# Loading keys and values over 128 partitions and regrouping the pooling and routing work of an attention and experts kernel

## The chip, the cores and the metric

The program runs on one core of a Trainium2 chip. The metric is the device time of one execution in microseconds. The core has five engines that run their own instruction queues in order: TensorE (PE in the profile, its weight loads PEld), VectorE (DVE), ScalarE (ACT), GpSimd (POOL) and SyncE (SP), which here only issues DMAs. Sixteen DMA engines move the data.

## What is computed

Attention with pooled keys and values, then a top-1 mixture of experts on its output. All tensors are float32.

```python
# q, k, v: batch 8, heads 8, sequence 576, head size 64; pool = 8, so 72 pooled keys
k_p = k.reshape(B, H, Sp, pool, D).mean(axis=3)
v_p = v.reshape(B, H, Sp, pool, D).mean(axis=3)
scores = scale * np.matmul(q, k_p.transpose(0, 1, 3, 2))
attn = softmax(scores)                      # max subtracted, sum + 1e-9
x = np.matmul(attn, v_p)                    # to 4608 tokens of 512
# experts: 8, hidden 1024
logits = x @ w_gate
expert_idx = np.argmax(logits, axis=1)      # gate_w: its softmax probability
out[mask] = gate_w[mask, None] * (np.maximum(x[mask] @ w1[e], 0) @ w2[e])
```

## The kernel before, in words

The program has two stages. `attention` computes x, finds the expert of each token and scatters the token rows, sorted by expert, to a DRAM tensor `xs` ("dispatched" in the profile). `experts`, which the change does not touch, reads these rows back in units of up to 512 tokens and multiplies them with the experts' weights, each split into a high and a low part.

Attention runs in 4 groups (g) of two batches each, and each group in 9 tiles of 128 tokens, so 36 tiles (t; i is the tile within the group). A group's k and v are each loaded in three thirds: `kv_load(g, i)` (L127 to L134) loads third i // 2 of k (i even) or v (i odd). The tile `raw` has 128 partitions of 3 x 512 floats, 786 KB in all: each partition holds 24 tokens of one head. Today this is two DMAs of 64 partitions on SP's queue, one for even and one for odd heads (`hp`), and four raw buffers are cycled. `kv_pool` (L136) adds up the 8 tokens of each pooled key in three halving adds: 128x768 (L141), 128x384 (L149) and then 64x192 into `kvp` for each hp (L146). Today GpSimd does thirds 0, 2, 3 and 5 of the next group in tiles 0 to 3, with VectorE doing the last add for hp = 1; VectorE does thirds 1 and 4 and all of group 0 but the third 3. VectorE's adds are cut into pieces in the list `halves`, of which one is taken at two points of each tile. `kv_transpose` (L156) turns a third of kvp on TensorE into the bank pm, and ScalarE copies it into kT and vT (L167, L169). `v_expand` multiplies v with a matrix that holds the identity and the gate weights, so that attention also yields each head's share of the router's logits.

A tile t of the loop does, in this order on each engine: transposes the weights P of tile t (`p_transpose`); `scores(t + 2)` on TensorE, then VectorE's row maximum mx (L224) and difference sd (L227); `q_transpose(t + 3)`; perhaps a kv_transpose or a v_expand; ScalarE's exp (`weights(t + 2)`, L232); `weigh(t)` on TensorE into the bank pU; `scale(t)` on VectorE: reciprocal (L264), logits lh (L266) and token rows xe (L268); `q_copy(t + 4)` on ScalarE (L207) from the loaded q tile `qa`. Between VectorE's operations `weave` takes steps from the list `steps`.

These steps are the routing. Tokens are routed in batches of three tiles (the last two batches have two tiles and one). When a batch's last tile is done (i = 2, 5, 8), `route` (L281) puts its steps on the list, one per weave: six that find the expert (L318, L319, L320, L322, L323 and `chosen`, L294, which also starts ScalarE's exp, L295), then the gate value (L327 to L329, L332), `before` (a count over earlier tokens on TensorE, L300 and L303, read by L305 and L306), the product pos x oh (L333), its sum (L334), and `put`: for each tile a cast to int32 (L312) and an indirect DMA of GpSimd that scatters 128 rows (L341). Tokens of the last batches ("late") go in another order.

Loads of the tile loop stand in SP's queue in program order: k and v of the next group at i = 0 to 3, its q halves at i = 4 and 7, its middle part qm at i = 4, and `clear_rows` (L363), four stores of 257 KB that blank the first rows of xs, just before the loop. In tiles 24 to 31 `w_split` (L355) splits expert 0's weights: ScalarE rounds a piece (L358), GpSimd subtracts (L359).

Before the loop stands the opening: loads of group 0, its pooling and transposes, the first scores. `warm(n)` issues n transposes of the identity to keep TensorE active while it waits; `WARM` lists the seven numbers.

Of the kernel before, what the change touches and what calls it, by code (L numbers as in the profile page):

```python
# [31 lines left out]
WARM = (14, 4, 4, 4, 18, 8, 8)  # L32
# [35 lines left out]
def attention(ctx, outer, tc, q, k, v, wg, w1v, w2v, xs, W, cst, carry, tab, banks):  # L68
# [9 lines left out]
    kraw = early.enter_context(tc.tile_pool(name="akv", bufs=4, side="right", reuse_waits="tile"))  # L78
# [48 lines left out]
    def kv_load(g, i):  # L127

        src, c0 = (v if i % 2 else k), 3 * (i // 2)
        raw = kraw.tile([P, 3, 512], F32, tag="raw", name=f"raw{g}_{i}")  # L130
        sv = src[2 * g : 2 * g + 2].rearrange("b (h4 hp) (k8 x) d -> hp (b h4) k8 (x d)", hp=2, k8=8)
        for hp in range(2):
            nc.sync.dma_start(out=raw[64 * hp : 64 * hp + 64], in_=sv[hp, :, :, c0 * 512 : c0 * 512 + 1536])
        raws[g, i] = raw  # L134

    def kv_pool(g, i, eng):  # L136

        raw, c0 = raws.pop((g, i)), 3 * (i // 2)

        def first():  # L140
            eng.tensor_tensor(out=raw[:, :, 0:256], in0=raw[:, :, 0:256], in1=raw[:, :, 256:512], op=ALU.add)  # L141

        def last(e, hp):
            r = slice(64 * hp, 64 * hp + 64)
            o = 64 - 64 * hp if i % 2 else 64 * hp
            e.tensor_tensor(out=kvp[r, c0 : c0 + 3, o : o + 64], in0=raw[r, :, 0:64], in1=raw[r, :, 64:128], op=ALU.add)  # L146

        def second():
            eng.tensor_tensor(out=raw[:, :, 0:128], in0=raw[:, :, 0:128], in1=raw[:, :, 128:256], op=ALU.add)  # L149
            last(eng, 0)  # L150
            if eng is nc.vector:
                last(eng, 1)

        return (first, second) if eng is nc.vector else (first, second, lambda: last(nc.vector, 1))

    def kv_transpose(g, i, bank, what="kv"):  # L156


        for c in range(3):
            nc.tensor.transpose(bank[:, c * P : (c + 1) * P], kvp[:, 3 * i + c, :], ident)  # L160
        m = bank[:, 0 : 3 * P].rearrange("p (c hp b k) -> p hp b k c", c=3, hp=2, b=8)
        for hp in range(2):
            rk, rv = slice(64 * hp, 64 * hp + 64), slice(64 - 64 * hp, 128 - 64 * hp)
            ko = kTs[g % 2].rearrange("p b j (hp k c) -> p hp (b j) k c", hp=2, c=9)
            vo = vT.rearrange("p b (j hp x) -> p hp (b j) x", j=4, hp=2)[:, :, :, 0:SK].rearrange("p hp b (k c) -> p hp b k c", c=9)
            if "k" in what:
                nc.scalar.copy(out=ko[rk, hp, :, :, 3 * i : 3 * i + 3], in_=m[rk, hp])  # L167
            if "v" in what:
                nc.scalar.copy(out=vo[rv, hp, :, :, 3 * i : 3 * i + 3], in_=m[rv, hp])  # L169
# [85 lines left out]
    def scale(t):  # L255

        u4 = (pS if t == NG * NT - 2 else pU)[:, :, 0 : 4 * VW].rearrange("p a (h x) -> p a h x", h=4)
        bt, (t0, _) = [(i, b) for i, b in enumerate(batches) if b[0] <= t][-1]
        i = t - t0
        if i == 0:  # L260
            xe[bt] = (p3.tile([P, NB, XR], F32, tag="xe", name=f"xe{bt}"), p2.tile([P, NB, H, NE], F32, tag="lh", name=f"lh{bt}"))
# [4 lines left out]
        nc.vector.tensor_tensor(out=lh[:, i].rearrange("p (a h) e -> p a h e", a=2), in0=u4[:, :, :, D : D + NE], in1=r.unsqueeze(3).to_broadcast([P, 2, 4, NE]), op=ALU.mult)  # L266
# [6 lines left out]
    steps, halves, ready, expands = [], [], [], []  # L273
# [7 lines left out]
    def route(bt):  # L281
# [5 lines left out]
        t1 = lambda s: p2.tile([P, NB], F32, tag=s, name=nm(s))[:, 0:nb]  # L287
        lg, d, ex, key, oh, pos = t8("rg"), t8("rd"), t8("rx"), t8("rk"), t8("ro", BF16), t8("rp")
        m, km, se, pf = t1("rm"), t1("rn"), t1("rs"), t1("rf")
        ix = p3.tile([P, NB], I32, tag="ix", name=nm("ix"))  # L290
        V = nc.vector

        def chosen():
            V.tensor_tensor(out=oh, in0=key, in1=bc(km), op=ALU.is_equal)  # L294
            nc.scalar.activation(out=ex, in_=d, func=AF.Exp)  # L295

        def before():
            bank = pq if expands else pm
# [11 lines left out]
        def put():  # L310
# [6 lines left out]
        steps.extend([  # L317
            lambda: V.tensor_reduce(out=lg, in_=lh.rearrange("p t h e -> p t e h"), axis=AX.X, op=ALU.add),  # L318
# [6 lines left out]
        ])  # L325
# [12 lines left out]
        steps.extend([before, row[1], gate[0], gate[1], row[2], gate[2], row[0], put] if t0 + nb + 3 >= NG * NT else [*gate, before, *row])  # L338
# [16 lines left out]
    def w_split(i):  # L355
# [3 lines left out]
        nc.gpsimd.tensor_tensor(out=W[:, a + 1, c], in0=raw, in1=f32(W[:, a, c]), op=ALU.subtract)  # L359
# [53 lines left out]
    for j in range(3):  # L413
        kv_load(1, j)
# [15 lines left out]
    *pooled, odd = kv_pool(0, 3, nc.gpsimd)  # L430
    run(kv_pool(0, 1, vec))
    warm(WARM[3])
    scores(0)
    kv_transpose(0, 0, pm, "v")
    weights(0)
    run(pooled)
    run(kv_pool(0, 5, vec))
    odd()
    warm(WARM[4])
    p_transpose(0)  # L440
    warm(WARM[5])
    kv_transpose(0, 2, pq, "v")
    kv_transpose(0, 1, pm, "v")
    q_copy(1)
    warm(WARM[6])
    v_expand(0, 0, pq)
    v_expand(0, 1, pm)
    q_transpose(1)
    q_copy(2)
    v_expand(0, 2, pPs[0])  # L450
    scores(1)
    v_expand(0, 3, pPs[1])
# [3 lines left out]
    late = {}  # L456
    clear_rows()
    for t in range(total):
        g, i = divmod(t, NT)
        more = g + 1 < NG  # L460
        if more:
            for j in {0: (0, 1, 2) if g else (), 1: (3,), 2: (4,), 3: (5,)}.get(i, ()):
                kv_load(g + 1, j)
            if i < 4:
                j = (0, 2, 3, 5)[i]
                *fs, late[j] = kv_pool(g + 1, j, nc.gpsimd)
                run(fs)
            for j in {1: (0, 1), 2: (2,), 3: (4,), 4: (3,), 5: (5,)}.get(i, ()):
                halves.extend([late.pop(j)] if j in late else kv_pool(g + 1, j, vec))
            if i == 4:  # L470
                q_load(g + 1, 0)
# [21 lines left out]
        if t + 2 < total:  # L493
            weights(t + 2)
        if t == total - 3:
# [5 lines left out]
        expands[:] = [t] if (more and i >= 7) or (g and i < 2) else []  # L501
# [14 lines left out]
        if t >= FIRST:  # L516
            scale(t)
        if t == total - 3:
            x_low()
# [746 lines left out]
```

## Time and profile before

| | |
|---|---|
| runs | 752.89, 758.91 and 757.84 us, median 757.84 |
| profiled execution | 751.57 us, of which the span that the trace covers is 749.2 |
| TensorE busy | 649.8 us, 87% of the span |
| VectorE, ScalarE, GpSimd busy | 358.8, 253.1 and 251.0 us |
| thirds of k and v | 48 DMAs of 384 KB |
| q halves | 8 DMAs of 1024 KB |

How to read it: times count from the start of the span. A window's busy times are sums over the instructions in it; the DMA share is the mean over 16 engines, so half of the engines always at work show as 0.5, and counts of overlapping packets can take it over 1. The granted clock is a share of TensorE's full 2.4 GHz. A wait is put down to what came last.

### The profile page before, as it was taken

The numbers are of one execution on the slowest core, as the hardware profiler recorded it, in microseconds if no ns is written. First come the engines' busy times: TensorE is split into PE (matmuls) and PEld (weight loads), VectorE is DVE, ScalarE is ACT, GpSimd is POOL, SyncE is SP. The second block draws the span as 40 slices with busy tenths as digits, with TensorE's granted clock in tenths as the row PEclk, the third lists the DMA queues.
The fourth block names the chain that finished last, engine by engine and source line by source line (L and its number), as shares of the span: only waits on it lengthen the run. The fifth ranks groups of instructions, "written<-read, shape, count | busy, mean of one in ns | idle before, by whom it ended". The sixth has DMA issues, their size and how long they took to land.

```text
span 749.2 us, 11594 instructions
## 1 busy us (share of the span) xinstructions
PE 649.8 (87%) x3702; PEld 568.3 (76%) x3702; DVE 358.8 (48%) x740; ACT 253.1 (34%) x482; POOL 251.0 (33%) x286
## 2 busy tenths in 40 slices
PE   2578897888879799998699989999999699999990
PEld 2577887877868588887598868898889678788980
DVE  3428789487876631245453632163315673122210
ACT  1135665646765120132362532052204352021100
POOL 6123356274653411043425521124123461101110
PEclk9999999899998999999899999999999999999996
DMA  4774958649632394144555752315323630300000
GB/s 114 186 216 157 202 218 181 197 165 258 195 113 82 113 279 162 42 138 147 183 165 179 229 162 64 101 45 180 110 86 92 200 101 10 100 16 31 31 31 15
DMA packets 58062, 99.23 MB, mean 132 GB/s; under 512 B 9678, under 2 KB 34254, under 8 KB 57936
## 3 DMA queue, kind: packets, MB, share of 16 engines
q1 hardware_dynamic: 49952, 77.14, 35.8%
q0 software_dynamic: 7440, 20.50, 7.6%
q8 instruction: 66, 1.08, 0.6%
q14 instruction: 60, 0.49, 0.2%
q10 hardware_dynamic: 544, 0.02, 0.0%
HBM read 75.57 MB, written 26.00 MB: 136 GB/s over the span
## 4 chain that ended last, share of the span: by engine, by line
PE 57%; issue 3%; DVE 2%; ACT 1%; DMA 1%; POOL 0%; ACTq 0%; DVEq 0%; SPq 0%; POOLq 0%
PE pU L772 28%; PE pP L741 18%; PE pq L741 9%; PE pS L708 2%; DVE H L870 1%; ACT W L916 1%; DVE W L922 1%; DMA dispatched<-xe,ix 1%; DVE H L854 0%; PE pm L699 0%; ACT X L899 0%; POOL out_dram L1098 0%; ACTq L642 0%; ACT H L849 0%; SPq L630 0%
## 5 line engine op out<-in xcount | busy, mean ns | idle before, releaser
L772 PE MATMUL pU<-W,H 128*128 128x512 f32 x912 | 218.9, 398 | 1.6 <-issue 1.6
L772 PEld LDWEIGHTS pU<-W,H 128*128 128x128 f32 x912 | 169.5, 188 | 41.1 <-issue 2.0
L741 PE MATMUL pP<-X,W 128*128 128x512 f32 (+3 forms) x760 | 149.6, 352 | 15.1 <-issue 9.9
L741 PEld LDWEIGHTS pP<-X,W 128*128 128x128 f32 x760 | 128.8, 194 | 31.0 <-issue 10.6
L1098 POOL DMA_INDIRECT out_dram<-Y,XE x51 | 50.6, 993 | 230.6 <-DVE Y L1017 202.3
L922 POOL TENSOR_TENSOR W<-ST,W 128x1024 fp32r<-128x1024 f32 x28 | 74.1, 2649 | 106.8 <-ACT W L916 106.6
L849 ACT ACTIVATE H<-pP 128x512 fp32r<-128x512 f32 x57 | 34.1, 599 | 185.2 <-PE pP L741 184.4
L1017 DVE TENSOR_SCALAR Y<-pU,XE 128x512 f32<-128x512 f32 x36 | 27.0, 749 | 133.2 <-PE pU L772 133.2
L870 DVE SCALAR_TENSOR_TENSOR H<-pP,H 128x512 fp32r<-128x512 f32 (+1 forms) x63 | 40.7, 646 | 92.3 <-ACT H L849 88.2
L252 PE MATMUL pU<-V,pt 128*128 128x146 f32 (+1 forms) x468 | 71.0, 313 | 13.7 <-DVE rn L323 10.3
L741 PE MATMUL pq<-X,W 128*128 128x512 f32 (+3 forms) x376 | 75.7, 350 | 4.6 <-DVE H L870 2.7
L252 PEld LDWEIGHTS pU<-V,pt 128*128 128x128 f32 (+1 forms) x468 | 65.1, 197 | 16.7 <-issue 8.3
L741 PEld LDWEIGHTS pq<-X,W 128*128 128x128 f32 x376 | 62.7, 191 | 12.9 <-DVE H L870 3.1
L916 ACT CAST W<-ST 128x1024 fp32r<-128x1024 f32 x56 | 57.2, 1050 | 0.0
L220 PE MATMUL pS<-kT,qT 128*128 128x144 f32 (+1 forms) x320 | 45.5, 297 | 2.1 <-DVE sd L227 2.1
L849 ACT ACTIVATE H<-pq 128x512 fp32r<-128x512 f32 x28 | 16.8, 599 | 87.3 <-PE pq L741 87.3
L141 POOL TENSOR_TENSOR raw<-raw 128x768 f32<-128x768 f32 x13 | 24.1, 1850 | 65.0 <-DMA raw<-in_v_dram 44.0
L922 DVE TENSOR_TENSOR W<-ST,W 128x1024 fp32r<-128x1024 f32 x28 | 42.3, 1509 | 6.0 <-ACT W L916 5.0
L220 PEld LDWEIGHTS pS<-kT,qT 128*128 128x128 f32 (+1 forms) x320 | 40.3, 184 | 4.1 <-issue 3.4
L341 POOL DMA_INDIRECT dispatched<-xe,ix x36 | 35.4, 984 | 13.1 <-POOL ix L312 8.1
L870 DVE SCALAR_TENSOR_TENSOR H<-pq,H 128x512 fp32r<-128x512 f32 (+1 forms) x30 | 19.8, 660 | 37.6 <-ACT H L849 37.2
L232 ACT ACTIVATE P<-sd 128x576 f32<-128x576 f32 x36 | 24.6, 684 | 34.4 <-DVE sd L227 30.7
(175 smaller groups left out, 717.5 us busy)
## 6 DMA issues: line engine op xcount, KB each, us to landing
ST<-in_moe_w_dram SPq DMA_DIRECT2D x56, 512.0 KB, 4.5
XE<-dispatched SPq DMA_DIRECT2D x52, 257.0 KB, 2.7
raw<-in_k_dram SPq DMA_DIRECT2D x24, 384.0 KB
raw<-in_v_dram SPq DMA_DIRECT2D x24, 384.0 KB
qa<-in_q_dram SPq DMA_DIRECT2D x8, 1024.0 KB
w<-in_moe_w_dram SPq DMA_DIRECT2D x8, 512.0 KB
dispatched<-empty SPq DMA_DIRECT2D x6, 257.0 KB
dispatched<-empty POOLq DMA_DIRECT2D x6, 257.0 KB, 7.6
```

What stands on the lines that cost most here:

```text
L220: nc.tensor.matmul(pS[p0 : p0 + n, j // 2, (j % 2) * 144 : (j % 2) * 144 + 144], lhsT=qT[t][:, j * P + p0 : j * P + p0 + n], rhs=kTs[g % 2 ...
L232: nc.scalar.activation(out=Ps[t % 2][:, :, 0:SK], in_=sds.pop(t).rearrange("p a h x -> p (a h) x"), func=AF.Exp, scale=1.0 / (8.0 * POOL))
L252: nc.tensor.matmul(pu[p0 : p0 + n, c // 3, (c % 3) * VW : (c % 3 + 2) * VW], lhsT=pt[t][c // 3][:, c % 3 * P + p0 : c % 3 * P + p0 + n], r ...
L341: apart(nc.gpsimd.indirect_dma_start(out=xs, out_offset=bass.IndirectOffsetOnAxis(ap=at, axis=0), in_=rows, in_offset=None))
L741: r = pe.matmul(out=pH[g % 3][:, :m], lhsT=w1s(w, f, k), rhs=x, start=i == 0, stop=i == len(passes) - 1)
L772: r = pe.matmul(out=pY[:, s % 2, :], lhsT=h, rhs=w[:, k * 512 : (k + 1) * 512], start=k + i == 0, stop=k == 7 and i == len(passes) - 1)
L849: act.activation(out=HH[:, f, o], in_=src[:, o], func=AF.Relu).then_inc(Q["A_h"], 1)
L870: return dve.scalar_tensor_tensor(out=dst[:, f, to], in0=src[:, at], scalar=0.0, in1=f32(HH[:, f, at]), op0=ALU.max, op1=ALU.subtract)
L916: act.copy(out=(W1H if i < 4 else W2H)[:, o], in_=ST[:, i, :]).then_inc(Q["A_s1" if i < 4 else "A_s2"], 1)
L922: eng.tensor_tensor(out=(W1L if i < 4 else W2L)[:, o], in0=ST[:, i, :], in1=f32((W1H if i < 4 else W2H)[:, o]), op=ALU.subtract).then_inc( ...
L1017: r = dve.tensor_scalar(out=Y[:, s, :], in0=a, scalar1=gate, scalar2=None, op0=ALU.mult)
L1098: pool.indirect_dma_start(out=out, out_offset=bass.IndirectOffsetOnAxis(ap=XE[u % 2][:, s, DM + 1 : DM + 2].bitcast(I32), axis=0), in_=Y[: ...
```

## The change

- `kv_load` makes one DMA of 128 partitions; partitions are now ordered batch, head, token part. There are five raw buffers.
- `kv_pool` makes three adds over 128 partitions, all on one engine. k stands in columns 0 to 63 of kvp and v in 64 to 127 for all heads, so ScalarE's copies to kT and vT move odd heads' k and even heads' v to the other 64 partitions.
- In the opening VectorE pools all thirds. In the loop it pools the thirds of k, GpSimd those of v, at i = 8 (two groups ahead), 2 and 5. Loads start earlier, and so do those of q.
- In `route`, for batches that are not late: four of the six steps run at once at the end of the batch's last tile, the exp follows the next tile's weights, the count follows its scaling, and three operations go to GpSimd (G). lh is stored with the heads innermost, as the reduction reads it.
- Weight splits with even i go from GpSimd to VectorE. `clear_rows` moves ahead, behind the first load of group 1. The fillers become 48 instead of 60.

```diff
-WARM = (14, 4, 4, 4, 18, 8, 8)
+WARM = (14, 6, 6, 4, 6, 6, 6)
...
-    kraw = early.enter_context(tc.tile_pool(name="akv", bufs=4, side="right", reuse_waits="tile"))
+    kraw = early.enter_context(tc.tile_pool(name="akv", bufs=5, side="right", reuse_waits="tile"))
...
-        sv = src[2 * g : 2 * g + 2].rearrange("b (h4 hp) (k8 x) d -> hp (b h4) k8 (x d)", hp=2, k8=8)
-        for hp in range(2):
-            nc.sync.dma_start(out=raw[64 * hp : 64 * hp + 64], in_=sv[hp, :, :, c0 * 512 : c0 * 512 + 1536])
+        sv = src[2 * g : 2 * g + 2].rearrange("b h (k8 x) d -> (b h k8) (x d)", k8=8)
+        nc.sync.dma_start(out=raw.rearrange("p c f -> p (c f)"), in_=sv[:, c0 * 512 : c0 * 512 + 1536])
...
+        def add(n):
+            out = kvp[:, c0 : c0 + 3, o : o + 64] if n == 64 else raw[:, :, 0:n]
+            return lambda: eng.tensor_tensor(out=out, in0=raw[:, :, 0:n], in1=raw[:, :, n : 2 * n], op=ALU.add)
+        return [add(n) for n in (256, 128, 64)]
...
-                nc.scalar.copy(out=ko[rk, hp, :, :, 3 * i : 3 * i + 3], in_=m[rk, hp])
+                nc.scalar.copy(out=ko[rk, hp, :, :, 3 * i : 3 * i + 3], in_=m[0:64, hp])
...
+        late = t0 + nb + 3 >= NG * NT
...
+        G = V if late else nc.gpsimd
...
-            lambda: V.tensor_copy(out=x[:, :, DM + 1].bitcast(I32), in_=cst["tok"][:, t0 : t0 + nb]),
-            lambda: V.tensor_scalar(out=se, in0=se, scalar1=1e-9, scalar2=None, op0=ALU.add),
+            lambda: G.tensor_copy(out=x[:, :, DM + 1].bitcast(I32), in_=cst["tok"][:, t0 : t0 + nb]),
+            lambda: G.tensor_scalar(out=se, in0=se, scalar1=1e-9, scalar2=None, op0=ALU.add),
...
-            lambda: V.tensor_tensor(out=pos, in0=pos, in1=oh, op=ALU.mult),
+            lambda: G.tensor_tensor(out=pos, in0=pos, in1=oh, op=ALU.mult),
...
+            run(pick[:4])
+            steps.append(lambda: run(pick[4:]))
+            powers.append(power)
+            def counted():
+                run([count, row[1], gate[1]])
+                steps.extend([lambda: run([gate[0], gate[2]]), row[2], lambda: run([row[0], put])])
+            counts.append(counted)
...
-        nc.gpsimd.tensor_tensor(out=W[:, a + 1, c], in0=raw, in1=f32(W[:, a, c]), op=ALU.subtract)
+        (nc.gpsimd if i % 2 else nc.vector).tensor_tensor(out=W[:, a + 1, c], in0=raw, in1=f32(W[:, a, c]), op=ALU.subtract)
...
-    for j in range(3):
+    kv_load(1, 0)
+    clear_rows()
+    for j in (1, 3):
         kv_load(1, j)
...
-            for j in {0: (0, 1, 2) if g else (), 1: (3,), 2: (4,), 3: (5,)}.get(i, ()):
+            for j in {1: (2,), 2: (4,), 3: (5,)}.get(i, ()) if g == 0 else {0: (3,), 1: (2,), 2: (4,), 3: (5,)}.get(i, ()):
                 kv_load(g + 1, j)
-            if i < 4:
-                j = (0, 2, 3, 5)[i]
-                *fs, late[j] = kv_pool(g + 1, j, nc.gpsimd)
-                run(fs)
-            for j in {1: (0, 1), 2: (2,), 3: (4,), 4: (3,), 5: (5,)}.get(i, ()):
-                halves.extend([late.pop(j)] if j in late else kv_pool(g + 1, j, vec))
+            if i == 2:
+                q_load(g + 1, 0)
...
-            if i == 7:
+            if i == 6:
                 q_load(g + 1, 1)
+        if g + 2 < NG and i >= 7:
+            kv_load(g + 2, i - 7)
+        G, j = (g + 2, 1) if i == 8 else (g + 1, {2: 3, 5: 5}.get(i, 1 if t == 0 else None))
+        if G < NG and j:
+            run(kv_pool(G, j, nc.gpsimd))
+        if more:
+            for j in {0: (0,), 3: (2,), 4: (4,)}.get(i, ()):
+                pieces.extend(kv_pool(g + 1, j, vec))
+            for _ in range((1, 1, 1, 2, 2, 2, 0, 0, 0)[i]):
+                halves.append(pieces.pop(0))
```

## Rows read from the trace of the kernel before

**Rows 1.** Windows; columns: stretch and length, busy us of each engine, TensorE's granted clock, DMA share, GB/s.
```profile
10.00:20.00 10.00, 1.76 (x7) 1.36 (x7) 4.42 (x13) 0.70 (x2) 3.38 (x24) 1.00 0.51 131
30.00:40.00 10.00, 6.25 (x41) 5.74 (x38) 3.74 (x6) 2.22 (x5) 3.40 (x3) 0.83 0.84 206
55.24:244.69 189.45, 160.39 (x1247) 151.50 (x1246) 149.64 (x367) 110.34 (x237) 94.37 (x103) 0.94 0.61 176
120.83:130.11 9.28, 9.05 (x80) 8.48 (x79) 7.94 (x26) 5.50 (x14) 4.42 (x5) 1.00 1.09 223
262.00:749.20 487.20, 447.34 (x2225) 380.29 (x2225) 178.71 (x270) 127.67 (x211) 129.70 (x95) 0.97 0.36 111
```

**Rows 2.** Timeline of the opening; columns: start, us, engine, line, operation, tile written<-read, count.
```profile
0.88 4.12 SPq L133 DMA_DIRECT2D raw<-in_k_dram  x6
...
11.56 0.96 DVE L141 TENSOR_TENSOR raw<-raw 128x768 f32<-128x768 f32 x1 [5.80 <-DMA raw<-in_k_dram]
...
22.98 0.96 DVE L141 TENSOR_TENSOR raw<-raw 128x768 f32<-128x768 f32 x1 [2.60 <-DMA raw<-in_k_dram]
...
41.36 0.96 DVE L141 TENSOR_TENSOR raw<-raw 128x768 f32<-128x768 f32 x1 [6.56 <-DMA raw<-in_v_dram]
...
45.03 7.16 SPq L365 DMA_DIRECT2D dispatched<-empty  x4
...
45.97 0.61 ACT L207 COPY qr<-qa 128x512 f32<-128x512 f32 x1
...
49.71 1.25 PE L220 MATMUL pS<-kT,qT 128*128 128x144 f32 x8
```

**Rows 3.** Timeline, VectorE's scaling of the first tile.
```profile
55.24 0.68 DVE L268 TENSOR_TENSOR xe<-pU,r 128x512 f32<-128x512 f32 x1
```

**Rows 4.** Waits from 52 to 250 us; columns: engine, tile, line, released by: total, times, longest.
```profile
POOL raw L141 <- DMA raw<-in_v_dram: 23.4, 5, 11.0
...
ACT qr L207 <- DMA qa<-in_q_dram: 8.4, 3, 3.7
...
PE pq L212 <- ACT qr L207: 7.1, 4, 3.2
...
POOL raw L141 <- DMA raw<-in_k_dram: 3.5, 1, 3.5
```

**Rows 5.** Timeline, VectorE and GpSimd, 101 to 105 us.
```profile
101.59 2.02 DVE L320 TENSOR_TENSOR rd<-rg,rm 128x24 f32<-128x24 f32 x1
...
101.73 1.82 POOL L141 TENSOR_TENSOR raw<-raw 128x768 f32<-128x768 f32 x1
...
103.64 0.99 POOL L149 TENSOR_TENSOR raw<-raw 128x384 f32<-128x384 f32 x1
...
104.71 0.58 POOL L146 TENSOR_TENSOR kvp<-raw 64x192 f32<-64x192 f32 x1
```

**Rows 6.** Timeline, VectorE and GpSimd, 199 to 225 us.
```profile
199.24 0.99 POOL L341 DMA_INDIRECT dispatched<-xe,ix  x1 [0.28 <-POOL ix L312]
...
200.70 0.97 POOL L341 DMA_INDIRECT dispatched<-xe,ix  x1 [0.28 <-issue]
...
201.52 4.87 DVE L320 TENSOR_TENSOR rd<-rg,rm 128x24 f32<-128x24 f32 x1
...
201.69 4.65 POOL L359 TENSOR_TENSOR W<-w,W 128x1024 fp32r<-128x1024 f32 x2
...
219.63 5.11 DVE L322 SCALAR_TENSOR_TENSOR rk<-rd,order 128x24 f32<-128x24 f32 x1
```

**Rows 7.** VectorE by line and form, 52 to 250 us; columns: count, busy us, mean ns.
```profile
L320 DVE TENSOR_TENSOR rd<-rg,rm 128x24 f32<-128x24 f32 x11 | 10.2, 923 | 0.0
L322 DVE SCALAR_TENSOR_TENSOR rk<-rd,order 128x24 f32<-128x24 f32 x11 | 8.5, 774 | 0.0
...
L320 DVE TENSOR_TENSOR rd<-rg,rm 128x16 f32<-128x16 f32 x1 | 0.2, 176 | 0.0
```

**Rows 8.** The page, costliest groups, one line.
```profile
L922 DVE TENSOR_TENSOR W<-ST,W 128x1024 fp32r<-128x1024 f32 x28 | 42.3, 1509 | 6.0 <-ACT W L916 5.0
```

More of the change, by code (lines that the diff above doesn't have):

```diff
@@ L130, in kv_load @@
         raw = kraw.tile([P, 3, 512], F32, tag="raw", name=f"raw{g}_{i}")
-        sv = src[2 * g : 2 * g + 2].rearrange("b (h4 hp) (k8 x) d -> hp (b h4) k8 (x d)", hp=2, k8=8)
-        for hp in range(2):
-            nc.sync.dma_start(out=raw[64 * hp : 64 * hp + 64], in_=sv[hp, :, :, c0 * 512 : c0 * 512 + 1536])
+        sv = src[2 * g : 2 * g + 2].rearrange("b h (k8 x) d -> (b h k8) (x d)", k8=8)
+        nc.sync.dma_start(out=raw.rearrange("p c f -> p (c f)"), in_=sv[:, c0 * 512 : c0 * 512 + 1536])
         raws[g, i] = raw
     def kv_pool(g, i, eng):
[L138 to L154, printed above, removed]
+        raw, c0, o = raws.pop((g, i)), 3 * (i // 2), 64 * (i % 2)
+        def add(n):
+            out = kvp[:, c0 : c0 + 3, o : o + 64] if n == 64 else raw[:, :, 0:n]
+            return lambda: eng.tensor_tensor(out=out, in0=raw[:, :, 0:n], in1=raw[:, :, n : 2 * n], op=ALU.add)
+        return [add(n) for n in (256, 128, 64)]
     def kv_transpose(g, i, bank, what="kv"):
@@ L166, in kv_transpose @@
             if "k" in what:
[L167 removed]
+                nc.scalar.copy(out=ko[rk, hp, :, :, 3 * i : 3 * i + 3], in_=m[0:64, hp])
             if "v" in what:
[L169 removed]
+                nc.scalar.copy(out=vo[rv, hp, :, :, 3 * i : 3 * i + 3], in_=m[64:128, hp])
     def v_expand(g, i, bank):
@@ L270, in scale @@
         weave(1, True)
-    steps, halves, ready, expands = [], [], [], []
+    steps, halves, ready = [], [], []
+    powers, counts = [], []
     def weave(n=1, half=False):
@@ L291, in route, with power, count @@
         V = nc.vector
+        G = V if late else nc.gpsimd
         def chosen():
             V.tensor_tensor(out=oh, in0=key, in1=bc(km), op=ALU.is_equal)
+            if late:
+                power()
+        def power():
             nc.scalar.activation(out=ex, in_=d, func=AF.Exp)
-        def before():
-            bank = pq if expands else pm
+        def count():
+            bank = pm
             nc.tensor.matmul(bank[:, 0 : nb * NE], lhsT=lstrict, rhs=oh.rearrange("p t e -> p (t e)"), start=True, stop=False, skip_group_check=True)
@@ L315, in put @@
                 ready.append(bt)
-        steps.extend([
-            lambda: V.tensor_reduce(out=lg, in_=lh.rearrange("p t h e -> p t e h"), axis=AX.X, op=ALU.add),
+        pick = [
+            lambda: V.tensor_reduce(out=lg, in_=lh, axis=AX.X, op=ALU.add),
             lambda: V.tensor_reduce(out=m, in_=lg, axis=AX.X, op=ALU.max),
@@ L336, in route @@
         ]
-        steps.extend([before, row[1], gate[0], gate[1], row[2], gate[2], row[0], put] if t0 + nb + 3 >= NG * NT else [*gate, before, *row])
+        if late:
+            steps.extend([*pick, count, row[1], gate[0], gate[1], row[2], gate[2], row[0], put])
+        else:
+            run(pick[:4])
[5 more added lines that the diff above has]
+            counts.append(counted)
     def scatter(at, rows):
@@ L429, in attention @@
     q_transpose(0)
-    *pooled, odd = kv_pool(0, 3, nc.gpsimd)
-    run(kv_pool(0, 1, vec))
     warm(WARM[3])
     scores(0)
-    kv_transpose(0, 0, pm, "v")
     weights(0)
[L436 to L443, printed above, removed]
+    for j in range(3):
+        run(kv_pool(0, 2 * j + 1, vec))
+        warm(WARM[4 + j])
+        kv_transpose(0, j, (pm, pq, pm)[j], "v")
+        if j == 0:
+            p_transpose(0)
     q_copy(1)
-    warm(WARM[6])
     v_expand(0, 0, pq)
-    v_expand(0, 1, pm)
+    v_expand(0, 1, pPs[0])
     q_transpose(1)
     q_copy(2)
-    v_expand(0, 2, pPs[0])
+    v_expand(0, 2, pm)
+    v_expand(0, 3, pPs[1])
     scores(1)
-    v_expand(0, 3, pPs[1])
     q_transpose(2)
@@ L455, in attention @@
     q_copy(3)
-    late = {}
-    clear_rows()
+    pieces = []
     for t in range(total):
@@ L494, in attention @@
             weights(t + 2)
+        run(powers)
+        powers.clear()
         if t == total - 3:
@@ L517, in attention @@
             scale(t)
+        for f in counts[:]:
+            counts.remove(f)
+            f()
         if t == total - 3:
```

10 lines of the change are left out of this document (4 added, 6 removed).

## The prediction, made before the changed kernel ran

> **What bounds the kernel now.** I read the busy shares first, then the windows by stage, then the timeline of the opening, then the waits and lines of VectorE and GpSimd in the tile loop. From 262 us to the end TensorE is busy 447.3 of 487.2 us [rows 1]: the experts are TensorE's, the change touches nothing there, and whatever ends earlier before it ends the kernel earlier by as much. So the question is the first 250 us, in two parts.
>
> The opening is bound by loads. Between 10 and 20 us TensorE works 1.8 of 10 us and almost only thirds of k are in flight, yet the DMA share is 0.51 at 131 GB/s [rows 1]. A half share for so long fits 8 engines of 16 that never rest. Each load here covers 64 partitions, and the outermost dimension of its source (b h4) is 8. VectorE starts on k's three thirds from 11.56 to 22.98 us, so 5.7 us apart, and on v's last at 41.36; tile 1's scores start at 49.71 [rows 2].
>
> The tile loop, from the first scaling of xe to the last, takes 189.45 us for 35 steps, 5.41 each, with TensorE busy 160.4 us [rows 1, 3]. Two undisturbed tiles in a row took 9.28 us, 4.64 each, TensorE busy for 9.05 of them [rows 1]. At that pace 35 steps take 162.4 us, so 27.0 us stand above TensorE's floor. I split them by the long steps. ScalarE waits 8.4 us for q, and TensorE 7.1 behind it [rows 4]. Two 24-column operations of VectorE take 4.87 and 5.11 us, the first beside two of GpSimd's weight splits (4.65 us); the quiet value is 0.18 [rows 6, 7], so 9.6 us. The other 10.3 I give to the same thing beside GpSimd's pooling: L320 at 2.02 us beside an add of 1.82 [rows 5]. Over the loop L320 and L322 average 0.92 and 0.77 us, eleven times each [rows 7].
>
> **The change, part by part.**
>
> Loads. One DMA per third, 128 partitions, source dimension 128: I expect all 16 engines. At the pace of the half share a full one gives 131/0.51 = 257 GB/s; a third (786 KB) takes 3.06 us, not 6.0. The nearest windows with a full share show 223/1.09 = 205 GB/s, with q's 1 KB runs among them [rows 1], and 206/0.84 = 245. First k today: 11.56 - 0.88 [rows 2] = 10.7 us, of which 6.0 are transfer and 4.7 start and landing. After: 0.88 + 4.7 + 3.1 = 8.6; k's last 14.7; q's middle part (0.26 MB) 1 us; v at 18.8, 21.9 and 24.9, where VectorE stands at 41.36 now. Five buffers take the wait for a free one from v's second third; its last reuses k's first, pooled long before. q's first half (1.05 MB at 205 GB/s) lands at 30.0. Today q_copy(1) starts at 45.97, 3.74 us before tile 1's scores [rows 2]; after, these start at 30.0 + 3.7 = 33.7, 16.0 us earlier. From v's side it would be 24.9 + (49.71 - 41.36) = 33.3, so q is just the later one. Bounds: at 200 GB/s 39.3, a gain of 10.4; at 300 about 30, a gain of 19.5. Value: -16.
>
> The Trainium skill (DMA: Bandwidth & Descriptors, section Bandwidth) gives 341 GB/s for a single load of 1 MB over 128 partitions; by that a third takes 2.3 us, six thirds 4.5 us less than I count, and q, which follows them, would land that much earlier. No row here shows a third of k on 16 engines, so my sum stays with the rows.
>
> First tiles. At -16 the first scaling is near 39 us. Behind q the queue carries its second half, group 1's first third (about 38 us: in time for tile 0's end), then the four cleared row blocks, moved ahead (1.05 MB, 4 us; today their issue takes 7.16 us at 45.03 [rows 2]), then four thirds at 45.4, 48.4, 51.5 and 54.6. Tile 3 wants the one of 51.5 at about 51.4, and the last v third lands at 62.7, just as GpSimd turns to it. +2, bounds 0 to +6.
>
> q earlier. Its halves move up by two tiles and one tile; each buffer has been read out by then, and the queue holds nothing that waits on them. The 7.1 us go: -7, bounds 0 and -8.4.
>
> Weight splits. Four of eight go to VectorE, where the same form takes 1.51 us [rows 8], in tiles 24 to 30, of which only the first three still pool. GpSimd never has two in a row, so a lock lasts 2.35 us at most. Of 9.6 us I take 5 as gone: bounds -9.6 and +2 (four splits in the chain, uncovered, would be +6, less half of the locks).
>
> Pooling and routing. GpSimd's adds go from twelve thirds to nine, in tiles 2, 5 and 8; its multiply, copy and add of routing leave VectorE, where each could be locked. Against that: a batch's three scatters, 1.46 us apart [rows 6], take 4.4 us, nearly a tile, and start at the end of tile 4. So the adds issued in tile 5 start near its end and run 1.82 + 0.99 + 0.58 = 3.4 us [rows 5], just where the batch's first four steps (L320 and L322 among them) are now issued in one lump. The tiles are separate on paper; by these durations they overlap. I take 3 of the 10.3 us, bounds -10 and +4. A new wait: VectorE's sum over pos waits for GpSimd's product, and behind it stands the next scaling, so TensorE. The product has about 4 us of slack after the adds, so nothing; up to 7 for each add that waits for its load as long as today's longest, 11.0 us [rows 4].
>
> At nothing: the one add over 128 partitions for two over 64, ScalarE's copies across partitions (same elements; ScalarE is busy 110 of 189 us [rows 1]), lh's order, exp behind the weights, 12 fewer filler transposes. These stand in TensorE's waits, and the granted clock was 0.83 in 30 to 40 us with them [rows 1], between its two levels, after idle time. Bounds together -3 and +3.
>
> Sum: -16 + 2 - 7 - 5 - 3 = **-29**. The profiled execution took 751.57 us (span 749.2), so 722.6. It lies 6.3 under the median of the runs, 757.84, and I put the forecast on the median's footing: 757.84 - 29 = **729**.
>
> **The rivals.**
>
> *The locks stay whole.* The overlap above costs what it did, with the W splits too: -16 + 2 - 7 = -21, 737. For it: the arithmetic of tiles 4 and 5. Against: three of the locked operations leave VectorE. The Trainium skill (SBUF — State Buffer, section Who interferes with whom) says that a VectorE instruction with two SBUF inputs and a GpSimd one that reads SBUF exclude each other for a whole instruction; the trace agrees (4.87 beside 4.65), and by that rule moving work between the two helps only where they don't meet in time.
>
> *The floor is reached.* All 27 us above TensorE's pace go: -16 + 2 - 27 = -41, 717. For it: VectorE is busy 149.6 us of 189 [rows 1] with its locks in that. Against: the same overlap.
>
> *The loads gain no rate.* The half share is the source's, not the engines'. Then v ends some 4 us earlier, from the fifth buffer alone, q and the splits give 12: -16, 742. Against: full shares at 205 GB/s and more.
>
> *Slower: VectorE waits for loads.* Today VectorE pools two thirds of a group and never waits for a load in the loop; GpSimd does, 23.4 + 3.5 = 26.9 us [rows 4], beside the chain. After, all three thirds of k are VectorE's, and each one late stops scaling and scores. With the rate of today all 26.9 us enter the chain: -4 - 7 + 27 = +16, 774. It decides from 29 us of such waits, 3.2 for each of nine thirds. Against: five buffers let loads run two tiles ahead.
>
> **How the numbers follow.** Forecast 0.50; locks whole 0.18; floor 0.14; no rate 0.12; slower 0.06. Range 711 to 744: it takes in the first four with the opening's bounds (-10 to -19.5) around the middle, and leaves out the slower case and the far ends. A change of this kernel shows from 1%, 7.6 us. The first four cases lie beyond that, their edges not quite: faster 0.91, within 1% 0.04, slower 0.05.
>
> **What would show it.** Right: a DMA share near 1 between 5 and 20 us; k's thirds some 3 us apart on VectorE; scores of tile 1 near 34 us; 35 steps in about 176 us; no wait of ScalarE for q; no operation of 24 columns above 2.5 us. Wrong: a share that stays near 0.5, thirds still 5 us apart, or VectorE listed as waiting for raw in the loop; and if the loop takes 189 us again though the opening is shorter, the step on locks has failed.

## The result, and the profile after

The changed kernel took 724.92 us (median of 5 runs, 721.39 to 726.15) beside 758.91 for the kernel before in the same comparison (752.89 to 770.25): a ratio of 0.961, 95% interval 0.957 to 0.965, 34 us less. The profiled execution took 721.39 us with a span of 719.7; the forecast on that footing was 722.6, on the median's 729. The total came out as forecast. Its terms did not.

I split the span at VectorE's scaling of token rows (xe): its first, its 35th, the end. Between the first and the 35th lie 34 steps. The prediction called this stretch 35 steps, a miscount: 189.45 us are 5.57 each, and TensorE's pace of 4.64 makes 157.8 of them, not 162.4. So 31.7 us stood above that floor, not 27.0.

| us | before | after | gain |
|---|---|---|---|
| to the first xe | 55.24 | 33.95 | 21.3 |
| 34 steps of the loop | 189.45 | 187.70 | 1.8 |
| from there to the end | 504.51 | 498.05 | 6.5 |

The opening gave more than forecast, the loop almost nothing. The windows after, with the columns of [rows 1]:

```profile
5.00:10.00 5.00, 1.21 (x9) 0.97 (x9) 4.90 (x14) 1.21 (x3) 4.84 (x12) 0.89 1.13 358
10.00:20.00 10.00, 7.68 (x42) 6.48 (x42) 5.08 (x8) 2.66 (x6) 5.43 (x29) 0.71 1.02 370
33.95:221.65 187.70, 156.59 (x1247) 150.20 (x1246) 139.46 (x331) 112.06 (x237) 85.88 (x122) 0.94 0.50 169
```

Where the share was 0.51 at 131 GB/s [rows 1] it is now 1.02 at 370. In the loop VectorE lost 10.2 us of work and GpSimd 8.5, yet its length stayed. The timeline of the opening, as in [rows 2]:

```profile
0.87 1.51 SPq L133 DMA_DIRECT2D raw<-in_k_dram  x3
...
5.67 1.49 DVE L142 TENSOR_TENSOR raw<-raw 128x768 f32<-128x768 f32 x2
...
7.49 0.96 DVE L142 TENSOR_TENSOR raw<-raw 128x768 f32<-128x768 f32 x1
...
10.00 1.87 DVE L142 TENSOR_TENSOR raw<-raw 128x768 f32<-128x768 f32 x2
...
17.83 0.76 DVE L217 TENSOR_TENSOR sd<-pS,mx 128x576 f32<-128x576 f32 x1
...
18.51 1.54 DVE L142 TENSOR_TENSOR raw<-raw 128x768 f32<-128x768 f32 x2
...
22.21 1.54 DVE L142 TENSOR_TENSOR raw<-raw 128x768 f32<-128x768 f32 x2
...
25.45 0.61 ACT L197 COPY qr<-qa 128x512 f32<-128x512 f32 x1
...
29.26 1.14 PE L210 MATMUL pS<-kT,qT 128*128 128x144 f32 x8
```

k's first third is pooled from 5.67 us (11.56 before), the thirds start 1.8 and 2.5 us apart, v's last starts at 22.21 (41.36), and tile 1's scores at 29.26 (49.71). VectorE takes v's thirds one right behind the other, 1.85 us apart, as soon as tile 0's sd (L217) is done. The loads no longer bound the opening from the first addition on. Before, up to 56 us, VectorE waited for them five times:

```profile
DVE raw L141 <- DMA raw<-in_k_dram: 12.3, 3, 5.8
DVE raw L141 <- DMA raw<-in_v_dram: 12.1, 2, 6.6
```

These 24.4 us are gone: after, up to 34 us, VectorE's list of waits has no such line, and ScalarE's copy of q (L197, at 25.45) doesn't wait for a load either.

The waits of the loop, in the form of [rows 4]:

```profile
PEld pm L150 <- POOL kvp L142: 12.1, 3, 4.1
...
PE pm L150 <- POOL kvp L142: 11.4, 3, 3.8
...
PE pm L389 <- DMA XE<-dispatched: 6.5, 1, 6.5
```

ScalarE's wait for q, 8.4 us before, is gone, and the wait of TensorE behind it has shrunk to under a microsecond. But TensorE now waits three times for thirds that GpSimd pooled too late, and once for the experts' first rows, which come back from `dispatched` (XE). The locked operations did not go either. VectorE by line and form, where L318 and L320 are the L320 and L322 of [rows 7]:

```profile
L318 DVE TENSOR_TENSOR rd<-rg,rm 128x24 f32<-128x24 f32 x11 | 11.5, 1046 | 0.3
L320 DVE SCALAR_TENSOR_TENSOR rk<-rd,order 128x24 f32<-128x24 f32 x11 | 7.1, 643 | 0.4
```

18.6 us in all, beside 18.7 before. But they stand elsewhere: the two operations in the tiles of the weight splits, 4.87 and 5.11 us before, are at 0.18, and all that is left stands beside adds. The timeline around the end of tile 5 shows why:

```profile
53.93 1.79 POOL L350 DMA_INDIRECT dispatched<-xe,ix  x1 [0.89 <-DVE xe L258]
...
56.21 1.20 POOL L350 DMA_INDIRECT dispatched<-xe,ix  x1 [0.28 <-POOL ix L310]
...
57.89 0.98 POOL L350 DMA_INDIRECT dispatched<-xe,ix  x1 [0.28 <-POOL ix L310]
...
58.46 2.29 DVE L318 TENSOR_TENSOR rd<-rg,rm 128x24 f32<-128x24 f32 x1
...
58.89 2.88 POOL L142 TENSOR_TENSOR raw<-raw 128x768 f32<-128x768 f32 x2
...
61.73 0.74 DVE L214 TENSOR_REDUCE mx<-pS 128x8 f32<-128x576 f32 x1
...
62.49 0.55 PE L150 MATMUL pm<-ident,kvp 128*128 128x128 f32 x3 [3.84 <-POOL kvp L142]
```

GpSimd takes its queue in order. Three scatters occupy it from 53.93 to 58.87; only then come the adds of v's third, at the very moment when VectorE does the next batch's first steps. L318 lasts 2.29 us where its quiet value is 0.18, the row maximum mx stands behind it in VectorE's queue until 61.73, and the transposes of that third wait 3.84 us. This stretch repeats in tiles 14 and 23: the steps behind tiles 5, 14 and 23 took 8.80, 9.68 and 9.10 us. The fourth long step is 12.88 us, behind tile 31:

```profile
201.23 1.08 POOL L350 DMA_INDIRECT dispatched<-xe,ix  x1 [1.21 <-DVE xe L330]
...
204.24 0.98 POOL L350 DMA_INDIRECT dispatched<-xe,ix  x1 [0.28 <-POOL ix L310]
...
207.87 1.76 SPq L384 DMA_DIRECT2D XE<-dispatched  x4
...
210.62 1.12 PE L389 MATMUL pm<-ident,XE 128*128 128x128 f32 x4 [6.51 <-DMA XE<-dispatched]
```

The new routing order issues the scatters of batch 9 ahead of the load of XE, which so waits for them and holds TensorE for 6.5 us.

### The profile page after: what moved, and what is told of

It reads as the page before. It is cut to its first block, busy times and chain, and to the rows that moved or that the text cites. A ratio compares the mean times of both kernels' runs of the same rounds, so it can differ in the third digit from the quotient of the medians.

```text
span 719.7 us, 11458 instructions
## 1 busy us (share of the span) xinstructions
PE 641.5 (89%) x3690; PEld 563.2 (78%) x3690; DVE 348.2 (48%) x702; ACT 255.1 (35%) x482; POOL 240.2 (33%) x300
## 4 chain that ended last, share of the span: by engine, by line
PE 59%; DVE 3%; issue 2%; ACT 1%; DMA 1%; ACTq 0%; POOL 0%; SPq 0%; POOLq 0%; DVEq 0%
PE pU L787 29%; PE pP L756 19%; PE pq L756 9%; PE pS L723 2%; DVE W L937 1%; ACT W L931 1%; DVE H L885 1%; DMA dispatched<-xe,ix 1%; DVE H L869 0%; PE pm L714 0%; ACT X L914 0%; ACTq L657 0%; POOL out_dram L1113 0%; DVE Y L1032 0%; ACT H L864 0%
## 5 line engine op out<-in xcount | busy, mean ns | idle before, releaser
L242 PE MATMUL pU<-V,pt 128*128 128x146 f32 (+1 forms) x468 | 66.4, 299 | 1.7 <-ACT pt L230 1.1
L242 PEld LDWEIGHTS pU<-V,pt 128*128 128x128 f32 (+1 forms) x468 | 61.3, 187 | 3.3 <-ACT pt L230 2.4
L350 POOL DMA_INDIRECT dispatched<-xe,ix x36 | 39.5, 1098 | 24.2 <-DVE xe L330 13.8
L214 DVE TENSOR_REDUCE mx<-pS 128x8 f32<-128x576 f32 x36 | 27.1, 752 | 24.5 <-PE pS L210 24.5
```

What stands on the lines that cost most here:

```text
L214: nc.vector.tensor_reduce(out=mx, in_=s4, axis=AX.X, op=ALU.max)
L242: nc.tensor.matmul(pu[p0 : p0 + n, c // 3, (c % 3) * VW : (c % 3 + 2) * VW], lhsT=pt[t][c // 3][:, c % 3 * P + p0 : c % 3 * P + p0 + n], r ...
L350: apart(nc.gpsimd.indirect_dma_start(out=xs, out_offset=bass.IndirectOffsetOnAxis(ap=at, axis=0), in_=rows, in_offset=None))
```

## The experiments

My theory: the loads give the gain, the early scatters take it back in the loop. The rivals: TensorE waits for the small routing operations that went to GpSimd; or the loop's gain went to something that the loads collide with.

**The width of one DMA.** The third as two DMAs again, of 64 partitions each, in the new partition order.

```diff
-        nc.sync.dma_start(out=raw.rearrange("p c f -> p (c f)"), in_=sv[:, c0 * 512 : c0 * 512 + 1536])
+        for hp in range(2):
+            r = slice(64 * hp, 64 * hp + 64)
+            nc.sync.dma_start(out=raw[r].rearrange("p c f -> p (c f)"), in_=sv[r, c0 * 512 : c0 * 512 + 1536])
```

> The changed kernel, but each third comes in two DMAs of 64 neighbouring partitions, whose source's outermost dimension is 64 (it was 8 in the kernel before). Theory A, the outermost dimension of 8 kept the loads on half of the engines: the two halves are as fast as the one load; DMA share near 1 from 10 to 20 us as after the change (1.02), tile 1's scores within 1.5 us of 29.26, time within 3 us of 725. Theory B, a load that covers 64 partitions gets half of the engines: share near 0.5, tile 1's scores at about 45 us (49.71 less some 4 for the fifth buffer), time about 741.

One run of 731.83 us; the first xe at 39.60, the loop 192.32. Windows of the opening, and a line of VectorE's waits up to 40 us:

```profile
5.00:10.00 5.00, 0.00 (x0) 0.00 (x0) 3.41 (x10) 0.52 (x1) 4.84 (x13) 0.89 1.04 213
10.00:20.00 10.00, 7.97 (x35) 6.80 (x36) 3.88 (x7) 2.68 (x7) 4.08 (x28) 0.50 1.08 217
```

```profile
DVE raw L144 <- DMA raw<-in_k_dram: 3.9, 3, 1.6
```

The share is full as with one DMA, yet 217 GB/s move instead of 370. Neither theory was met: the share is A's, the time lies between the two. So the change of the load did two things: with the new order of partitions the share went from a half to a whole (131 to 217 GB/s), and the 128 partitions in one DMA did the rest. By the first xe (39.60 and 33.95) the second is worth 5.7 of the opening's 21.3 us, in this one run. The other 15.6 us aren't split: the new order of partitions, the fifth buffer and the new order of work in the opening came together. The Trainium skill (SBUF — State Buffer, section "Can I just issue two DMAs to hit both halves?") says no to its own heading's question: two loads to the two halves run one after the other. Its table of partition ranges, above that section, gives about 218 GB/s as the limit of 64 partitions. The 213 and 217 here agree with that figure; no window here shows whether the two DMAs run one after the other.

**GpSimd's adds one tile earlier**, so that they stand ahead of the scatters in its queue.

```diff
-        if g + 2 < NG and i >= 7:
-            kv_load(g + 2, i - 7)
+        if g + 2 < NG and i in (6, 7):
+            kv_load(g + 2, i - 6)
...
-        G, j = (g + 2, 1) if i == 8 else (g + 1, {2: 3, 5: 5}.get(i, 1 if t == 0 else None))
+        G, j = (g + 2, 1) if i == 7 else (g + 1, {1: 3, 4: 5}.get(i, 1 if t == 0 else None))
```

> GpSimd's adds are issued one tile earlier (i = 1, 4, 7 in place of 2, 5, 8), so ahead of a batch's scatters and not behind them. Theory, the adds come too late: TensorE's 11.4 us of waiting for the last v third in tiles 6, 15 and 24 go, and the two-input steps of VectorE at the end of tiles 2, 5, 8 (L318 at 1.05 us on the mean) no longer meet an add; the loop of 35 steps falls from 187.7 us by 9 to 15, time 710 to 716. Rival, the adds only meet other work (VectorE's own pooling, the scatters that now come later): L318 falls, other two-input lines rise, the loop falls by 3 us or less, time 722 to 725.

708.56 us, ratio 0.935 (0.927 to 0.943); the loop 171.91, 15.8 less, so somewhat more than the theory expected. Lines and timeline:

```profile
L320 DVE SCALAR_TENSOR_TENSOR rk<-rd,order 128x24 f32<-128x24 f32 x11 | 4.2, 383 | 0.4
L318 DVE TENSOR_TENSOR rd<-rg,rm 128x24 f32<-128x24 f32 x11 | 2.0, 182 | 0.3
```

```profile
50.88 2.89 POOL L142 TENSOR_TENSOR raw<-raw 128x768 f32<-128x768 f32 x2
...
55.94 1.71 POOL L350 DMA_INDIRECT dispatched<-xe,ix  x1 [0.92 <-POOL ix L310]
...
60.25 0.18 DVE L318 TENSOR_TENSOR rd<-rg,rm 128x24 f32<-128x24 f32 x1
```

With the adds ahead of the scatters L318 is at its quiet value in all eleven batches, and no transpose waits for a third from GpSimd. No instruction is new or gone. The loads of two thirds moved up with the adds, but GpSimd waits for loads in the loop no less than in the changed kernel (18.9 us beside 15.7); so the 16 us come from the order in GpSimd's queue.

**The rows of batch 9 held back** behind the load of XE, with XE given the first place in its memory pool (first run), and without that (second run).

```diff
-                steps.extend([lambda: run([gate[0], gate[2]]), row[2], lambda: run([row[0], put])])
+                steps.extend([lambda: run([gate[0], gate[2]]), row[2], row[0] if bt == AHEAD + 1 else lambda: run([row[0], put])])
+                if bt == AHEAD + 1:
+                    kept.append(put)
...
             x_open()
+            run(kept)
```

> Batch 9's three scatters are issued after the load of the first 512 token rows and not before it, and these rows get the memory that comes free first. Theory, TensorE's wait of 6.5 us for XE in step 31 is a new one that the faster tiles uncovered, and it is on the path: 5 to 6.5 us less, time 718.5 to 720. Rival, the stretch to the end of attention is set by the last scatters, which are now later: 1.5 us less at most, or up to 3 us more.

> The changed kernel with batch 9's scatters behind the load of the first rows, but these rows in their old place in memory (the one difference to the run that moved both, whose loop was 6.6 us shorter and whose time after the loop was 6.5 us longer). Theory 1, the place in memory lengthened the experts: the loop is 3 to 6 us shorter than 187.7, the time after it stays at 495 to 497, in all 717 to 721. Theory 2, holding the scatters itself lengthens what follows: 722 to 724, with 501 us after the loop.

722.28 us (721.20 to 723.47) with XE moved, 715.48 (714.62 to 716.84) without. TensorE's wait for XE goes in both. The loop is 179.72 us in the second run, 8.0 shorter than after, and 181.05 in the first, where the time behind the 35th xe, 504.5 us beside 498.1 after, took it back. The first run met neither of its values. The second lies below Theory 1's 717, and its time behind the 36th xe is 496.4, so Theory 2 falls. The wait was worth about 9 us by the medians; moving XE in memory goes with about 7 us more, for a reason that I haven't found (last section).

**The three small operations back on VectorE**, all else as after.

```diff
-        G = V if late else nc.gpsimd
+        G = V
```

> The changed kernel with the three small routing operations (product, copy, add) back on VectorE, everything else as changed. Theory 1, the loss of the new order lies in GpSimd's queue, where the early scatters stand ahead of the adds: nothing changes, 722 to 727. Theory 2, it lies in the handover (GpSimd stands 44.1 us before the product L331 and 13.5 before L327): 715 or less. Theory 3, the handover was worth something, since VectorE's short operations are locked again: 728 to 735.

723.49 us (721.00 to 724.12), loop 189.61: no difference, as Theory 1 expected. With the adds as late as after, the handover to GpSimd isn't what the loop pays for.

**Adds early and rows held, with XE moved.** The edits of the two experiments above together.

> GpSimd's adds one tile earlier and batch 9's scatters held back until the first rows are read, both in one kernel. Theory, two separate waits: the gains add up in the loop (15.8 and 6.6 us by the profiles), time 702 to 705, and what is then left above 693 (some 10 us) belongs to the order of the steps itself. Rival, the rows' wait only covers slack further on: 707 to 710.

708.23 us (704.77 to 711.44), the rival's value; loop 170.29: the two don't add up. TensorE still waits 3.1 us for XE there. The time says less than the loop, since XE is moved here too.

**The routing order of before**, with all else of the change: steps taken singly between operations, scatters at the end of the list.

```diff
-            run(pick[:4])
-            steps.append(lambda: run(pick[4:]))
-            powers.append(power)
...
+            steps.extend([*pick, *gate, count, *row])
```

> The changed kernel with the routing of the kernel before: one step per weave, all small operations on VectorE, the exp started right behind the choice, the count in the list. Theory 1 (the prediction's value): the new order is worth some 3 us, time 726 to 730. Theory 2, the lump of four steps meets GpSimd's adds as the single steps did and the new order is worth nothing or costs: time 719 to 725. Theory 3, the new order is what took undisturbed tiles from 4.64 to about 4.05 us: the loop is 10 us longer or more, time 735 and above.

693.02 us (690.98 to 694.86), ratio 0.914 (0.906 to 0.922), 32 us less than after. None of the three theories came near: all took the new order to cost 6 us at most. The loop, and its two lines (L317 and L319 there):

```profile
34.09:192.67 158.58, 148.77 (x1247) 141.76 (x1246) 135.36 (x361) 110.82 (x237) 79.92 (x92) 1.00 0.58 199
```

```profile
L317 DVE TENSOR_TENSOR rd<-rg,rm 128x24 f32<-128x24 f32 x11 | 4.8, 438 | 0.0
L319 DVE SCALAR_TENSOR_TENSOR rk<-rd,order 128x24 f32<-128x24 f32 x11 | 2.0, 180 | 0.0
```

158.58 us are 4.66 a step: TensorE's pace of [rows 1], 4.64, is reached. The granted clock is 1.00 of the full 2.4 GHz over the whole stretch where its mean was 0.94 after, and TensorE's busy time is shorter with it, 148.8 us for the same 1247 matmuls instead of 156.6.

**Adds early on top of that**, by the edit of the second experiment.

> The kernel with the old routing, and GpSimd's adds one tile earlier. Theory, the early adds only helped because the new order puts the scatters ahead of them; with the old order the scatters come later anyway: 691 to 695. Rival, the earlier place is better in itself, since it keeps the adds from VectorE's pooling: 685 to 690.

693.64 us (690.21 to 694.51), loop 158.23: nothing. The place of the adds matters only beside early scatters.

**Loads alone**: the new loads, five buffers and the new opening, with before's places of pooling, q, splits, routing steps and `clear_rows`; the last add of GpSimd's thirds, half VectorE's before, is GpSimd's. Its core, against the change:

```diff
-        G, j = (g + 2, 1) if i == 8 else (g + 1, {2: 3, 5: 5}.get(i, 1 if t == 0 else None))
-        if G < NG and j:
-            run(kv_pool(G, j, nc.gpsimd))
+        if more and i < 4:
+            run(kv_pool(g + 1, (0, 2, 3, 5)[i], nc.gpsimd))
```

> The loads of the change (one DMA per third, five buffers, new opening, evictions that shift partitions), with routing, the places of loads and of pooling in the loop, q's loads and the weight splits as before; GpSimd does its four thirds whole. Theory 1, the prediction's values (q 7, splits 5) and nothing for the pooling: 12 us above the kernel with the old routing (693), so 703 to 708. Theory 2, the pooling's new places are worth a lot by themselves: 715 or more. Theory 3, faster loads already take away the waits in the loop: 693 to 699.

713.97 us (713.41 to 715.26), ratio 0.950 (0.940 to 0.960). That is 11 us less than the whole change takes (724.92). Theory 2 is the nearest: before's places of pooling cost more than the prediction's values allow. The first xe at 34.07, the loop 179.43. There is no wait of ScalarE for q, though q's loads stand where they stood. The locks are whole:

```profile
L317 DVE TENSOR_TENSOR rd<-rg,rm 128x24 f32<-128x24 f32 x11 | 12.2, 1109 | 0.0
L319 DVE SCALAR_TENSOR_TENSOR rk<-rd,order 128x24 f32<-128x24 f32 x11 | 10.8, 982 | 0.0
```

**q's loads at their old place**, in the kernel with before's routing.

```diff
-            if i == 2:
-                q_load(g + 1, 0)
             if i == 4:
+                q_load(g + 1, 0)
                 qm_load(g + 1)
-            if i == 6:
+            if i == 7:
```

> The kernel with the old routing (693 us), and q's halves loaded at i = 4 and 7 again. Theory 1, the earlier place is worth the 7.1 us that TensorE waited before: 699 to 701. Theory 2, the faster loads in front of q clear the queue and q comes in time from its old place: 692 to 695.

693.22 us (690.33 to 694.21): nothing, as Theory 2 expected. The waits for q went because the loads ahead of q became short, not because q moved.

**All weight splits on GpSimd**, same base.

```diff
-        (nc.gpsimd if i % 2 else nc.vector).tensor_tensor(out=W[:, a + 1, c], in0=raw, in1=f32(W[:, a, c]), op=ALU.subtract)
+        nc.gpsimd.tensor_tensor(out=W[:, a + 1, c], in0=raw, in1=f32(W[:, a, c]), op=ALU.subtract)
```

> The kernel with the old routing (693 us), and all eight weight splits on GpSimd again. Theory 1, the prediction's value: 5 us slower, 697 to 700. Theory 2, both double locks of 4.87 and 5.11 us come back whole: 701 to 704. Theory 3, without waits before them GpSimd's splits no longer come in pairs: 692 to 695.

704.32 us (701.64 to 707.35), 11.3 more, close to Theory 2; the loop 168.12, 9.5 more. The long operations of [rows 6] are back, twice:

```profile
157.27 5.25 DVE L317 TENSOR_TENSOR rd<-rg,rm 128x24 f32<-128x24 f32 x1
...
176.99 5.11 DVE L319 SCALAR_TENSOR_TENSOR rk<-rd,order 128x24 f32<-128x24 f32 x1
```

```profile
157.83 4.65 POOL L359 TENSOR_TENSOR W<-w,W 128x1024 fp32r<-128x1024 f32 x2
...
177.39 4.65 POOL L359 TENSOR_TENSOR W<-w,W 128x1024 fp32r<-128x1024 f32 x2
```

With the splits shared one lock is left, 2.67 us beside a single split of 2.36.

**Four buffers** instead of five, same base.

```diff
-    kraw = early.enter_context(tc.tile_pool(name="akv", bufs=5, side="right", reuse_waits="tile"))
+    kraw = early.enter_context(tc.tile_pool(name="akv", bufs=4, side="right", reuse_waits="tile"))
```

> The kernel with the old routing, and four raw buffers. Theory, the fifth buffer matters little once loads are fast: k's first buffer is free before the queue reaches the load that wants it, 693 to 697. Rival, it is what lets loads run ahead in the loop: 702 and above.

695.62 us (694.42 to 699.50), 2.6 more, with a loop of 158.13, which is no longer than with five, and the first xe at 34.23: the 2.6 us lie behind the loop, where executions differ as much without any edit (last section). With the wide loads the fifth buffer is worth next to nothing.

## Why the prediction was right in its total and wrong in its terms

From before to after the runs make a chain in which each kernel has one part more, and its loop tells what the part was worth there: before 189.45; loads alone 179.43 (-10.0); pooling moved to its new places, with its loads, q's and `clear_rows`, 168.12 (-11.3); splits shared 158.58 (-9.5); new routing order 187.70 (+29.1). What a part was worth holds in this order of adding them. The two loops in the middle, loads alone and then all splits on GpSimd:

```profile
34.07:213.50 179.43, 156.26 (x1247) 150.10 (x1246) 141.57 (x348) 111.20 (x237) 91.41 (x99) 0.94 0.51 177
33.44:201.56 168.12, 153.07 (x1247) 145.81 (x1246) 139.16 (x357) 111.17 (x237) 89.00 (x96) 0.97 0.55 189
```

- **Opening, -16.** Right that the loads bound it, but too small: tile 1's scores came 20.5 us earlier, the first xe 21.3. The first fault is the rate. I scaled the half share to 257 GB/s; it is 358 to 370. The Trainium skill (DMA: Bandwidth & Descriptors, section Bandwidth) gives 341 GB/s for 1 MB over 128 partitions, there issued from GpSimd; the two windows here lie 5 and 8.5% above it. By that figure the sum would have been -20.5. The second fault is the path. The sum let tile 1's scores wait for q's first half, landing at 30.0, or for v's last third. After the change neither is waited for: v's thirds stand behind tile 0's scores on VectorE, and the copy of q stands at 25.45 with no wait. So it is luck that the sum by the skill's figure meets the measurement. The bounds, -10.4 to -19.5, stood on 200 and 300 GB/s and left the measured 20.5 out.
- **First tiles, +2.** Nothing showed. No wait of VectorE for raw stands in the list of the loop; the one late third, for which GpSimd waits 15.7 us, is off the chain. With that the slower rival, VectorE waiting for loads, falls; the rival by which loads gain no rate fell with the 370 GB/s.
- **q earlier, -7.** The waits went, as said, but for another reason. Loads alone remove them; q at its old place costs nothing. The step that failed is the one that gave the gain to moving q.
- **Weight splits, -5.** Right in direction, half the size: 9.5 us in the loop. In the changed kernel the double locks are gone whole. In the pair of runs that differ in the splits alone, 5.25 and 5.11 us went and one of 2.67 came, so 7.5 us of locks for 9.5 of the loop: the four splits on VectorE, 1.2 us each there and not the 1.51 that I took, left no cost that shows. The sign named for it was met: no operation of 24 columns is above 2.5 us after, the longest is the 2.29 shown.
- **Pooling and routing, -3 (-10 to +4).** This step failed. It put two edits into one number, and in the loop they are of opposite sign. The new places of pooling gave 11.3 us (the locks of the two lines fell from 23.0 us with loads alone to 14.3), and the new routing order cost 29.1, so +18 together, far outside the bounds. The overlap was named (scatters of nearly a tile, the adds behind them, the lump of steps beside them), and it is just what the timeline shows; but I priced it by the time that the locks held already, and not by what waits behind: the locked operation stands in VectorE's queue ahead of the next mx, and the late third holds up TensorE's transposes in front of the next scores. That is 16 us, by the adds moved one tile. The gain of the pooling's new places has no run of its own; q's place costs nothing, the places of the loads and of `clear_rows` weren't tried alone.
- **A wait that I did not see.** The new order puts batch 9's scatters ahead of the load of XE. I followed the queues for loads of k, v and q and for GpSimd's adds, but not to the experts' first load, which depends on the same DRAM tensor. 8.0 us of the loop by the rows held back.
- **Loads, beyond the opening.** The chain's first link, -10.0 in the loop, holds q's 7.1 us, whose waits are gone there; no run takes the other 2.9 apart.
- **TensorE's own time.** The floor of 4.64 us was read where the granted clock was 1.00; over the loop of before its mean was 0.94. Along the chain TensorE was busy 160.4, 156.3, 153.1, 148.8 and 156.6 us for the same 1247 matmuls, at 0.94, 0.94, 0.97, 1.00 and 0.94. So 7.8 of the new order's 29.1 us are TensorE's own busy time at the lower clock. The prediction split the time above the floor by waits alone and had no term for this.
- **The end, at nothing.** 6.5 us of the profiled pair lie behind the 35th xe, in stages that the change leaves alone. Profiles of one and the same experts' code lie that far apart (below), so this is no effect that I can give to the change.

So -21.3, -1.8 and -6.5 make the -29.5 of the profiled pair, beside -29 forecast: too little credited to the opening, too much to the loop. That the total agrees is luck, since the faults cancel. My own sign of failure was met: "the loop takes 189 us again though the opening is shorter". It took 187.70. Of the rivals the one with the locks whole (737) says most of what happened in the loop, though the splits' share of them did go.

What stays open: of the new order's 29.1 us, adds early and rows held together give back 17.4 (187.70 to 170.29). Of the remaining 11.7, 5.3 are TensorE's busy time (154.1 us at a mean granted clock of 0.97, beside 148.8 at 1.00). In the same stretch VectorE's reciprocal (L330) waits for GpSimd's small addition, 9.1 us in seven waits, with the next scaling behind it, and TensorE still 3.1 us for XE; whether the small operations on VectorE would recover it was tried only with late adds, where they changed nothing.

The best version found is the change with before's routing order: 693.02 us, 0.956 of the change's median, and it beats both kernels.

## What to carry to other kernels

When a change reorders an in-order queue, list for each engine what ends up behind the moved instruction and who waits for that, down to the next stage's first load; a lock or a late result costs what is queued behind it, not only its own length. Price edits that act on the same operations one by one: the single term of -3 here held +29 and -11. And a total that agrees proves none of its terms: split the span at a marker that both kernels have, then undo the edits singly.

## What the runs showed of the hardware that was not expected

**A full share is not a full rate.** At 10 to 20 us the three forms of the same load show 0.51 at 131 GB/s (64 partitions, outer source dimension 8), 1.08 at 217 (64 partitions, outer dimension 64) and 1.02 at 370 (128 partitions in one DMA). The share says that engines have packets under way, not how fast these move; the column of GB/s must be read beside it. The Trainium skill (DMA: Bandwidth & Descriptors, section Why a DMA increments its semaphore by 16 and not by 1) takes the number of engines from a common divisor of the outermost dimensions of source and destination, at most 16. By that 8 gives 8 engines and 64 gives 16, as the shares of 0.51 and 1.08 show; the prediction had the first of these from the row alone, and had not separated it from the number of partitions.

**Unchanged code that takes 6 us more.** From the 36th xe to the end the profiles show two lengths: 495.2 to 498.5 us in ten of them and 501.2 to 502.3 in four (before, both kernels with XE moved, and all splits on GpSimd). The last has the same experts and the same memory as the kernel that it is an edit of, and its other runs were up to 5.7 us shorter than the profiled one. Here are the windows of 20 us from 120 us, and 40 us from 320 us, behind the 36th xe, first for splits on GpSimd, then for before's routing order:

```profile
324.45:344.45 20.00, 15.71 (x80) 15.65 (x81) 7.89 (x12) 7.34 (x10) 9.38 (x7) 0.83 0.66 199
524.45:564.45 40.00, 32.94 (x172) 28.29 (x171) 26.37 (x39) 17.08 (x28) 21.50 (x12) 0.89 0.47 147
```

```profile
315.55:335.55 20.00, 18.24 (x96) 18.27 (x97) 10.23 (x14) 7.93 (x11) 11.31 (x7) 0.91 0.66 212
515.55:555.55 40.00, 33.20 (x174) 28.73 (x173) 27.40 (x38) 17.19 (x28) 23.89 (x13) 0.91 0.46 147
```

In the first window TensorE does 80 matmuls instead of 96, at a granted clock of 0.83 instead of 0.91; at 96 in 20 us, 16 matmuls are some 3.3 of the 5.5 us (an estimate). Where the rest arises I haven't settled. With XE moved four executions of four took 721 to 724 us, without it 715 to 717, so its place seems to favour the longer form; but with adds early as well two of four were at 711 and two at 705, and a kernel that doesn't move it shows the longer form too. The cause is open.
